# Attention scores with 64 rows of contraction for each head, and a changed row maximum, scale computation and order, in a fused attention and mixture kernel

## The chip, the cores and the metric

The kernel runs on one core of a Trainium2 chip. The metric is the time of one execution on the device, in microseconds; the time of a version is the median of several runs.

## The reference

Inputs are q, k and v of 4 batches, 12 heads, 448 tokens and 64 channels, two vectors `g_q` and `g_k` of 64, and two pairs of weight matrices (768 x 2048 and 2048 x 768). All is float32.

```python
def rmsnorm(x, g):
    return x / sqrt(mean(x * x, -1) + 1e-6) * g

scores = 0.125 * rmsnorm(q, g_q) @ rmsnorm(k, g_k).T      # for each batch and head: 448 x 448
attn = softmax(scores)                                   # over the last axis
x = (attn @ v), heads side by side                       # 1792 tokens x 768

h = x @ w_in;   g = h * clip(h + 3, 0, 6) / 6;  y = g @ w_out       # first feed-forward
h = y @ w_in2;  g = max(h, 0) ** 2;             out = g @ w_out2    # second
```

## The kernel before

**Order of work.** The program is written out by a planner. Every piece of work is a task with a key (its wished place), one or several engines that could do it, each with a cost in ns, the tasks before it and the buffers it uses; the planner simulates the engines and writes the instructions in the order that it finds. The tables at the top (`STEPS` for the place of each pair of heads, `SCALE`, `VMAX`, `LOOK`, `FROM`, `EVERY`) set the keys, and `CLASSES` the number of buffers of each size. Each engine runs its instructions in the order written, and waits by semaphores. SP issues the DMAs.

**Attention.** The work goes by 24 pairs of heads (batch `j`, pair `p`). For each pair `norms` loads q and k of both heads side by side, 128 partitions x 14 rows of 64 (`qk`), squares them (`sq`), sums the squares (`ss`), makes 1/rms on POOL (`rs`), multiplies (L509, L513) and splits the result in two float16 numbers, a high half (L526 on ScalarE, L530 on VectorE) and a low half that is the rest (L534). Both go to `src`, where each row of 128 columns is 64 high and 64 low. A DMA transpose turns `src` into `T`: on partitions 0 to 63 the high halves, on 64 to 127 the low halves, the tokens along the columns. `W` is a copy of the queries' part of `T` with the two halves of partitions exchanged, by two DMAs (L610, L611). For the first pair the transposes are three: `W` comes from a third one (L562) of a copy of `src` in reversed order.

The scores of a pair are 2 x 448 rows, in seven blocks of 128 rows. A block takes two matmuls over 128 contraction rows, `T` with `T` (high by high and low by low) and `W` with `T` (high by low and low by high), L722. The block in the middle holds rows of both heads, 64 of each, and takes two matmuls for each half. VectorE takes the negative row maximum of the block from PSUM (L729) and multiplies it by a factor `esc` (L739; after each block in batch 0, after two in the others, `GROUP`). ScalarE takes the exponential with `esc` as scale and this as bias, and sums the rows (L682). In eleven pairs of the first two batches (`ACROSS`) TensorE then transposes the exponentials in float32 (L692), they are copied back (L699) and multiplied by v in float32 (L799). In the others they are split in high and low halves (L753, L759), transposed by DMA (L767) and multiplied by v's halves in float16 (L818). The result, split again, is `x`.

**Feed-forward.** The first one runs on the 448 tokens of a batch at a time, in units of 18 matmuls of 128 x 128 by 448 columns (L1192, three float16 products for each float32 one), with the gate by L1224, L1227, L1256 and L1262. The second runs on two batches at a time, by seven products over sums of blocks (L1446, L1536). Weights are loaded, split, scaled and stored in a scratch area in DRAM, from which they are read again.

**Scales.** Before a split a value is multiplied by a power of two. `scale_of` makes it: the maximum of a column over partitions (by a TensorE transpose, L362, and a reduce, L365), its exponent kept by a mask and a floor (`pow2_floor`, L338, L339), the two factors from it (L369, L370), spread to all partitions by a small matmul (L373) and kept by a copy on either engine (L376, L379). There are 37 of these.

## Time and profile before

| what | before |
|---|---|
| median of 3 runs | 1136.13 us (1133.94 to 1138.83) |
| profiled execution | 1130.28 us, of which the span of the trace is 1128.5 |
| TensorE busy | 1050.0 us (93%), mean granted clock 0.985 |
| VectorE busy | 893.3 us (79%) |
| ScalarE busy | 770.7 us (68%) |
| GpSimd (POOL) busy | 102.2 us (9%) |

The profile is of one execution, a little under the median. Busy times are shares of the whole span and mix stretches with different limits; the rows below show them by stretch. A matmul's duration is longer than its distance to the next one, since matmuls are pipelined: distances between starts tell its cost. The same holds, less strongly, for VectorE.

### The profile page before, as it was taken

To read this page: it belongs to the slowest core of one execution; us is meant where nothing else is said; L and a number is where in the kernel's file an instruction comes from. 1 tells how busy PE (TensorE), PEld (TensorE's weight loads), DVE (VectorE), ACT (ScalarE), POOL (GpSimd) and SP (SyncE) were. 2 spreads that over 40 slices of the span, in tenths; PEclk is the share of its full clock that TensorE was granted. 3 is DMA by queue.
4 is the path that set the end of the run, shared out by engine and by line. 5 is a ranking of instruction groups with operands and counts; after the bars stand their busy time and mean duration, and the time that the engine had idled before them with its cause. 6 is when DMAs were issued, how large, how long until landed. Compare 5 with 4: busy or idle time off the path is not lost.

```text
span 1128.5 us, 17054 instructions
## 1 busy us (share of the span) xinstructions
PE 1050.0 (93%) x5765; PEld 542.5 (48%) x5765; DVE 893.3 (79%) x1952; ACT 770.7 (68%) x1480; POOL 102.2 (9%) x143
## 2 busy tenths in 40 slices
PE   1589999889999999999999999999889999999998
PEld 0255555435544554445445445454444545555554
DVE  6999989999999977799669989887889961116940
ACT  1799779899699756577458867787865656564620
POOL 3411211202202220021000000000000000000000
PEclk9699999899999999999999999999999999999999
DMA  9965557669999999999998899888765654323343
GB/s 244 248 174 175 133 168 257 188 186 272 297 284 228 242 242 208 253 222 213 200 330 312 302 317 353 307 262 273 242 201 166 225 189 126 116 91 128 113 161 105
DMA packets 235719, 246.90 MB, mean 219 GB/s; under 512 B 139392, under 2 KB 188672, under 8 KB 235632
## 3 DMA queue, kind: packets, MB, share of 16 engines
q1 hardware_dynamic: 235568, 245.68, 75.1%
q8 instruction: 45, 0.74, 0.3%
q14 instruction: 42, 0.34, 0.1%
q0 software_dynamic: 64, 0.13, 0.1%
HBM read 162.76 MB, written 45.61 MB: 185 GB/s over the span
## 4 chain that ended last, share of the span: by engine, by line
PE 54%; DVE 25%; DMA 10%; ACT 6%; issue 3%; SPq 1%; POOL 1%; ACTq 0%; DVEq 0%
PE m L1192 19%; PE ps_s L722 3%; DVE nm L729 3%; PE mo_0A L1536 2%; PE ps_a L799 2%; PE mo_1A L1536 2%; PE mo_2A L1536 2%; PE ps_s L692 2%; DMA spill_o<-wc_out 2%; DVE wc_in L1010 2%; PE mo_2C L1536 2%; DVE g L1262 2%; DMA qk<-in_qk_dram 2%; DVE wc_out L1010 1%; PE ps_r L785 1%
## 5 line engine op out<-in xcount | busy, mean ns | idle before, releaser
L1192 PEld LDWEIGHTS <-ws 128*128 128x128 f16 x2304 | 221.8, 98 | 225.5 <-issue 20.0
L1192 PE MATMUL m<-x,ws 128*128 128x448 f16 x1152 | 236.1, 355 | 7.7 <-DVE gr L1227 5.4
L1192 PE MATMUL m<-g,ws 128*128 128x448 f16 x1152 | 235.8, 354 | 6.7 <-DMA ws<-spill 4.4
L1446 PEld LDWEIGHTS <-wi 128*128 128x128 f16 x1008 | 98.8, 98 | 97.2 <-issue 5.7
L1536 PEld LDWEIGHTS <-wo 128*128 128x128 f16 x1008 | 98.3, 98 | 98.1 <-issue 5.4
L682 ACT ACTIVATE e<-ps_s,nm,esc 128x448 f32<-128x448 f32 x168 | 121.2, 724 | 26.3 <-DVE nm L739 24.7
L729 DVE TENSOR_REDUCE nm<-ps_s 128x1 f32<-128x448 f32 x168 | 102.4, 614 | 3.1 <-PE ps_s L722 2.8
L1483 ACT ACTIVATE go<-gq,g_s 128x448 f16<-128x448 f32 x104 | 62.7, 658 | 39.8 <-DVE gq L1499 27.1
L1489 DVE SCALAR_TENSOR_TENSOR go<-gq,g_s,go 128x448 f16<-128x448 f32 x112 | 71.1, 676 | 0.7 <-ACT go L1483 0.5
L692 PE MATMUL ps_s<-eye,e 128*112 128x128 f32 x308 | 49.1, 292 | 16.5 <-ACT e L682 16.1
L722 PE MATMUL ps_s<-T 128*128 128x448 f16 (+1 forms) x192 | 62.8, 377 | 0.2 <-DVE w_s L379 0.2
L722 PE MATMUL ps_s<-T,W 128*128 128x448 f16 (+1 forms) x192 | 62.3, 371 | 0.5 <-DMA W<-T 0.5
L759 DVE SCALAR_TENSOR_TENSOR p<-e,su,p 128x448 f16<-128x448 f32 x91 | 59.1, 677 | 2.1 <-ACT p L753 1.8
L1224 ACT ACTIVATE t<-m,half,six 128x448 f32<-128x448 f32 x64 | 45.6, 719 | 18.3 <-PE m L1192 18.0
L475 POOL TENSOR_TENSOR rs<-ss,mhalf 128x14 f32<-128x14 f32 x21 | 57.5, 2738 | 1.8
L753 ACT ACTIVATE p<-e,su 128x448 f16<-128x448 f32 x73 | 46.4, 663 | 12.4 <-DVE su L668 4.3
L692 PEld LDWEIGHTS ps_s<-eye,e 128*112 128x112 f32 x308 | 35.6, 140 | 36.7 <-ACT e L682 28.3
L1462 ACT ACTIVATE gq<-gq 128x448 f32<-128x448 f32 x56 | 31.9, 570 | 21.1 <-DVE gq L1391 20.6
L1536 PE MATMUL mo_0A<-go,wo 128*128 128x448 f16 x192 | 42.0, 352 | 4.3 <-DVE go L1489 4.3
L1227 DVE SCALAR_TENSOR_TENSOR gr<-t,m 128x448 f32<-128x448 f32 x64 | 39.0, 611 | 8.2 <-ACT t L1224 8.1
L1256 ACT ACTIVATE g<-gr,d 128x448 f16<-128x448 f32 x62 | 39.8, 665 | 6.6 <-DVE gr L1227 6.5
L474 POOL TENSOR_SCALAR ss<-ss 128x14 f32<-128x14 f32 x21 | 7.9, 374 | 388.8 <-DVE ss L445 334.2
(329 smaller groups left out, 1950.4 us busy)
## 6 DMA issues: line engine op xcount, KB each, us to landing
ws<-spill SPq DMA_DIRECT2D x66, 384.0 KB, 4.8
wi<-spill_i SPq DMA_DIRECT2D x48, 384.0 KB, 3.8
wo<-spill_o SPq DMA_DIRECT2D x42, 384.0 KB, 3.2
wr<-in_w1i_dram SPq DMA_DIRECT2D x16, 768.0 KB, 4.9
wr_in<-in_w2i_dram SPq DMA_DIRECT2D x16, 768.0 KB, 6.7
...
```

Source lines behind the costliest of these rows:

```text
L475: nc.gpsimd.tensor_tensor(r, ss, mhalf, op=ALU.pow)
L682: nc.scalar.activation(tl(ve)[:, r % 2], tl(vps)[:, 0:S], AF.Exp, bias=sums["nm"][:, r:r + 1], scale=esc, accum_out=sums["su"][:, r:r + 1])
L692: nc.tensor.transpose(o[:, c], tl(ve)[:, r % 2, c * VR:(c + 1) * VR], eye)
L722: nc.tensor.matmul(ps[at:at + z - a, 0:S], q_[:, a:z], ks[:, h * S:(h + 1) * S], start=(i == 0), stop=(i == 1))
L729: nc.vector.tensor_reduce(sums["nm"][:, r:r + 1], tl(vps)[:, 0:S], axis=AX.X, op=ALU.max, negate=True)
L753: nc.scalar.activation(tl(vp)[:, r % 2, 0], tl(ve)[:, r % 2], AF.Copy, scale=sums["su"][:, r:r + 1])
L759: nc.vector.scalar_tensor_tensor(tl(vp)[:, r % 2, 1], tl(ve)[:, r % 2], sums["su"][:, r:r + 1], tl(vp)[:, r % 2, 0], op0=ALU.mult, op1=ALU ...
L1192: nc.tensor.matmul(tl(vph)[:, 0:S], w[:, wa, k], tl(rhs[k])[:, xa], start=(first_ and k == 0 and c == 0), stop=(last and k == nf - 1 and c ...
L1446: nc.tensor.matmul(tl(vph)[:, 0:S], w[:, wa, k0 + k], tl(vo)[:, to, xa], start=(starts and k == 0 and x == 0), stop=(k == KH - 1 and x == ...
L1483: nc.scalar.activation(tl(vo)[:, 0], tl(v_), AF.Copy, scale=up)
L1489: nc.vector.scalar_tensor_tensor(tl(vo)[:, 1], tl(v_), up, tl(vo)[:, 0], op0=ALU.mult, op1=ALU.subtract)
L1536: nc.tensor.matmul(tl(vph)[:, 0:S], w[:, g, wa, kk], tl(ops[y])[:, xa], start=(starts and k0 + k + y == 0 and z == 0), stop=(k0 + k + y == ...
```

## The change

**Scores.** `src` and `T` now hold the high halves and the low halves in 1024 columns each, and the two heads of a pair lie on partitions 0 to 63 and 64 to 127. A score block contracts the 64 rows of its head in three matmuls: high by high, high by low, low by high (low by low is left out). Two blocks of 128 rows, one of each head, are one task of six matmuls into two PSUM tiles; the last group has 64 rows of each head in one tile. There is no `W`, and the first pair has two transposes. A transpose moves 2048 columns where it moved 1792.

```diff
+        full = n // P
+        rows = [[(h, i * P, i * P + P, 0, i * P)] for i in range(full) for h in range(2)] + [[(h, full * P, n, h * D, full * P) for h in range(2)]]
...
-            def swap():
-                nc.sync.dma_start(tl(vW)[0:D], tl(vT)[D:P, 0:NR])
-                nc.sync.dma_start(tl(vW)[D:P], tl(vT)[0:D, 0:NR])
...
-                for h, a, z, at, _ in rows[r]:
-                    for i, q_ in enumerate(qs):
-                        nc.tensor.matmul(ps[at:at + z - a, 0:S], q_[:, a:z], ks[:, h * S:(h + 1) * S], start=(i == 0), stop=(i == 1))
...
+                    for i, (qa, ka) in enumerate(((0, 0), (0, 1), (1, 0))):
+                        for x in pair:
+                            for h, a, z, at, _ in rows[x]:
+                                e = slice(h * D, h * D + D)
+                                q0 = 8 * P * qa + (MAIN + P + D if h else MAIN + 2 * P if a < MAIN else -MAIN)
+                                k0 = 8 * P * ka + (D if h else P)
+                                nc.tensor.matmul(tl(vpss[x])[at:at + z - a, 0:S], T[e, q0 + a:q0 + z], T[e, k0:k0 + S], start=(i == 0), stop=(i == 2))
```

To fill the new `src`, the split writes four pieces for a pair where it wrote one: two of 2 x 3 x 64 = 384 columns and two of 2 x 64 = 128 (the last rows are written twice).

```diff
-            s, x = flat_src()
-            nc.vector.tensor_tensor(s[:, :, D:P], x, s[:, :, 0:D], op=ALU.subtract)
...
+            for x, hi, l in pieces(t0, t1):
+                nc.vector.tensor_tensor(l, x, hi, op=ALU.subtract)
```

**Row maximum.** One instruction now reads the score tile, multiplies it by `esc` (which has become negative), writes the product back over the tile and keeps the minimum of each row. The multiplication of the maximum is gone, and the exponential takes a constant scale of -1. All 168 blocks go this way, and each instruction is followed by one that reads the accumulator.

```diff
-                nc.vector.tensor_reduce(sums["nm"][:, r:r + 1], tl(vps)[:, 0:S], axis=AX.X, op=ALU.max, negate=True)
+                x = tl(vps)[:, 0:S]
+                nc.vector.tensor_tensor_reduce(x, x, nought.to_broadcast([P, S]), esc, 3e38, ALU.add, ALU.min, sums["nm"][:, r:r + 1])
...
-                nc.vector.tensor_scalar(nm, nm, esc, None, op0=ALU.mult)
...
-                nc.scalar.activation(tl(ve)[:, r % 2], tl(vps)[:, 0:S], AF.Exp, bias=sums["nm"][:, r:r + 1], scale=esc, accum_out=sums["su"][:, r:r + 1])
+                nc.scalar.activation(tl(ve)[:, r % 2], tl(vps)[:, 0:S], AF.Exp, bias=sums["nm"][:, r:r + 1], scale=-1.0, accum_out=sums["su"][:, r:r + 1])
```

**Scales.** Both factors come from one instruction (a mask, and an exclusive or with a constant pair), and the product with another constant pair, on VectorE, takes the place of the copy. The floor is a constant column beside the values, set once on POOL. Where a scale is for a sum (`total`), two instructions stay ahead of it.

```diff
-            pow2_floor(pw, a)
-            nc.vector.tensor_scalar(pair[:, 0:1].bitcast(I32), pw.bitcast(I32), -1, (268 - shift) << 23, op0=ALU.mult, op1=ALU.add)
-            nc.vector.tensor_scalar(pair[:, 1:2], pw, 2.0 ** (shift - 14), None, op0=ALU.mult)
+                nc.vector.tensor_scalar(a, a, 2.0 ** -87, None, op0=ALU.max)
+            nc.vector.scalar_tensor_tensor(pair.bitcast(I32), a.bitcast(I32).to_broadcast([1, 2]), 0x7F800000, flip2.bitcast(I32), op0=ALU.bitwise_and, op1=ALU.bitwise_xor)
...
-        def keep_a():
-            nc.scalar.copy(box[:, 1:3], tl(vps)[:, P:P + 2])
...
-            nc.vector.tensor_copy(box[:, 1:3], tl(vps)[:, P:P + 2])
+            nc.vector.tensor_tensor(box[:, 1:3], tl(vps)[:, P:P + 2], by2[shift], op=ALU.mult)
```

**Smaller parts.** The maxima of v are taken over 128 partitions x 1344 columns where it was 112 x 1536; the low half of v of a pair is one instruction where it was two; the factor of the norms' vectors is made behind the first sum of squares.

**Order.** All numbers of the tables are new, the costs of some tasks too (the exponential 640 where 704 stood), and there is one buffer of class A less and two of class H less.

```diff
-SCALE = (0.9368554078568024, 1.125097042654467, 0.5862702874871, 0.7879065098910517)
+SCALE = (1.0381251219859378, 0.7855009702768905, 0.198882525895536, 2)
...
-CLASSES = {"A": 14, "H": 50, "B": 3, "wr": 3, "w": 8, "ps": 8}
+CLASSES = {"A": 13, "H": 48, "B": 3, "wr": 3, "w": 8, "ps": 8}
```

How the rows stand on TensorE at the first scores of the program, pair 0_0 (`ps_s_0_0_0` is its block 0, and the last number of a name is that of the value). Before:

```order
L722 LDWEIGHTS T_0_0_249
L722 MATMUL ps_s_0_0_0_304<-T_0_0_249 128x448
L722 LDWEIGHTS W_0_0_257
L722 MATMUL ps_s_0_0_0_304<-T_0_0_249,W_0_0_257 128x448
L722 LDWEIGHTS T_0_0_249
L722 MATMUL ps_s_0_0_1_307<-T_0_0_249 128x448
L722 LDWEIGHTS W_0_0_257
L722 MATMUL ps_s_0_0_1_307<-T_0_0_249,W_0_0_257 128x448
```

The same place in the changed program:

```order
L690 LDWEIGHTS T_0_0_287
L690 MATMUL ps_s_0_0_0_346<-T_0_0_287 128x448
L690 LDWEIGHTS T_0_0_287
L690 MATMUL ps_s_0_0_1_348<-T_0_0_287 128x448
L690 LDWEIGHTS T_0_0_287
L690 MATMUL ps_s_0_0_0_346<-T_0_0_287 128x448
L690 LDWEIGHTS T_0_0_287
L690 MATMUL ps_s_0_0_1_348<-T_0_0_287 128x448
L690 LDWEIGHTS T_0_0_287
L690 MATMUL ps_s_0_0_0_346<-T_0_0_287 128x448
L690 LDWEIGHTS T_0_0_287
L690 MATMUL ps_s_0_0_1_348<-T_0_0_287 128x448
```

Block 0 and block 1 (one of each head) now alternate, and each takes three matmuls where it took two of twice the contraction rows.

On VectorE, at the first row maxima of pair 0_0 (`nm` holds the maxima; `qk_0_2` and `src_0_2` belong to the norms of pair 0_2). Before:

```order
L729 TENSOR_REDUCE nm_0_0_323<-ps_s_0_0_0_304 128x1
L513 TENSOR_TENSOR qk_0_2_233<-qk_0_2_233,gg_70 128x448
L445 TENSOR_REDUCE ss_0_3_332<-sq_0_3_321 128x14
L739 TENSOR_SCALAR nm_0_0_323<-nm_0_0_323,esc_73 128x1
L729 TENSOR_REDUCE nm_0_0_323<-ps_s_0_0_1_307 128x1
L534 TENSOR_TENSOR src_0_2_334<-qk_0_2_233,src_0_2_334 128x14x64
L739 TENSOR_SCALAR nm_0_0_323<-nm_0_0_323,esc_73 128x1
```

In the changed program:

```order
L699 ISA ps_s_0_0_0_346,nm_0_0_374<-ps_s_0_0_0_346,nought_76,esc_73 128x448
L699 ISA nm_0_0_374 128x1
L512 TENSOR_TENSOR qk_0_2_275<-qk_0_2_275,rs_0_2_318 128x896
L699 ISA ps_s_0_0_1_348,nm_0_0_374<-ps_s_0_0_1_348,nought_76,esc_73 128x448
L699 ISA nm_0_0_374 128x1
L516 TENSOR_TENSOR qk_0_2_275<-qk_0_2_275,gg_70 128x448
```

The product with `esc` no longer stands some instructions behind the maximum; the reading of the accumulator stands directly behind each.

On ScalarE, ahead of the gate of unit 5 of the first feed-forward's first batch (`t_5`; `e_1_3_0` is an exponential of pair 1_3, `ws`, `wf`, `wr` are weights in work). Before:

```order
L973 ACTIVATE ws_9_1912<-wf_9_1527,w0_8_s_123 128x768
L526 CAST src_1_5_1924<-qk_1_5_1757 128x14x64
L682 ACTIVATE e_1_3_0_1929,su_1_3_1849<-ps_s_1_3_0_1834,nm_1_3_1848,esc_73 128x448
L682 ACTIVATE e_1_3_0_1929,su_1_3_1849<-ps_s_1_3_1_1837,nm_1_3_1848,esc_73 128x448
L1224 ACTIVATE t_5_1950<-m_5_1851,half_75,six0_140 128x448
```

In the changed program:

```order
L644 ACTIVATE e_1_2_0_1797,su_1_2_1751<-ps_s_1_2_0_1737,nm_1_2_1750 128x448
L933 ACTIVATE ws_8_1809<-wf_8_1466,w0_8_s_127 128x768
L933 ACTIVATE ws_9_1821<-wf_9_1516,w0_8_s_127 128x768
L644 ACTIVATE e_1_2_0_1797,su_1_2_1751<-ps_s_1_2_1_1739,nm_1_2_1750 128x448
L1184 ACTIVATE t_4_1833<-m_4_1768,half_75,six0_144 128x448
L862 ACTIVATE wr_10_1497<-wr_10_1497 128x768
L872 ACTIVATE wf_10_1831<-wr_10_1497 128x768
L862 ACTIVATE wr_11_1602<-wr_11_1602 128x768
L1184 ACTIVATE t_5_1862<-m_5_1800,half_75,six0_144 128x448
```

The gate of unit 5 now stands behind the first exponentials of pair 1_2, where it stood behind those of pair 1_3.

## Rows read from the trace of the kernel before

**Rows 1.** Busy time by stretch: length, five engines (instructions), granted clock, DMA share, GB/s.

```profile
0.00:60.00 60.00, 24.87 (x101) 12.62 (x101) 48.81 (x105) 29.92 (x58) 22.23 (x35) 0.83 0.89 232
60.00:300.00 240.00, 221.25 (x1321) 121.00 (x1320) 227.34 (x544) 206.92 (x411) 40.61 (x54) 0.98 0.70 206
300.00:690.00 390.00, 381.08 (x2132) 192.08 (x2131) 333.00 (x758) 277.93 (x517) 39.41 (x54) 1.00 0.99 263
690.00:1129.00 439.00, 422.76 (x2218) 216.83 (x2216) 284.16 (x548) 255.91 (x496) 0.00 (x0) 1.00 0.56 185
```

**Rows 2.** Waits of the run: who waits for whom, us in total, times, longest.

```profile
ACT e L682 <- DVE nm L739: 24.7, 24, 3.5
...
PE m L1192 <- DVE gr L1227: 5.4, 1, 5.4
```

**Rows 3.** Timeline of TensorE from 396 us: start, duration, instruction.

```profile
396.10 0.54 PE L1192 MATMUL m<-g,ws 128*128 128x448 f16 x2
396.48 0.35 PE L722 MATMUL ps_s<-T 128*128 128x448 f16 x1
396.67 0.35 PE L722 MATMUL ps_s<-T,W 128*128 128x448 f16 x1
396.86 0.35 PE L1192 MATMUL m<-g,ws 128*128 128x448 f16 x1
```

**Rows 4.** Timeline of TensorE around a value product of halves.

```profile
343.08 1.31 PE L1192 MATMUL m<-x,ws 128*128 128x448 f16 x6
344.31 0.38 PE L818 MATMUL ps_a<-pt_1A,v 128*64 128x448 f16 x1
344.32 0.38 PE L818 MATMUL ps_a<-pt_1B,v 128*64 128x448 f16 x1
344.53 0.35 PE L818 MATMUL ps_a<-pt_1A,v 128*64 128x448 f16 x1
...
346.23 0.35 PE L818 MATMUL ps_a<-pt_1B,v 128*64 128x448 f16 x1
346.52 0.36 PE L1192 MATMUL m<-x,ws 128*128 128x448 f16 x1
```

**Rows 5.** Groups of VectorE by form: out<-in and count, then busy us, mean ns.

```profile
L729 DVE TENSOR_REDUCE nm<-ps_s 128x1 f32<-128x448 f32 x168 | 102.4, 614 | 3.1 <-PE ps_s L722 2.8
L759 DVE SCALAR_TENSOR_TENSOR p<-e,su,p 128x448 f16<-128x448 f32 x91 | 59.1, 677 | 2.1 <-ACT p L753 1.8
L534 DVE TENSOR_TENSOR src<-qk,src 128x896 f16<-128x896 f32 x23 | 24.9, 1081 | 2.3 <-ACT src L526 2.3
L1065 DVE TENSOR_TENSOR wq_in<-wq_in 128x384 f32<-128x384 f32 x32 | 17.7, 554 | 0.4
...
L1459 DVE SCALAR_TENSOR_TENSOR gq<-gq 128x448 f32<-128x448 f32 x8 | 5.0, 621 | 0.0
L1459 DVE DVE_READ_ACCUMULATOR gq<-gq 128x1 f32 x8 | 0.7, 85 | 0.0
```

**Rows 6.** Timeline of VectorE from 114 us: a row bias, a row maximum, the next.

```profile
114.35 0.21 DVE L739 TENSOR_SCALAR nm<-nm,esc 128x1 f32<-128x1 f32 x1
114.47 0.61 DVE L729 TENSOR_REDUCE nm<-ps_s 128x1 f32<-128x448 f32 x1
115.01 1.08 DVE L445 TENSOR_REDUCE ss<-sq 128x14 f32<-128x896 f32 x1
```

**Rows 7.** Timeline of VectorE from 24 us: the steps of a scale, the next.

```profile
24.38 0.14 DVE L338 TENSOR_SCALAR v_s<-v_s 1x1 int32<-1x1 int32 x1
...
24.86 1.06 DVE L445 TENSOR_REDUCE ss<-sq 128x14 f32<-128x896 f32 x1
```

**Rows 8.** Groups of ScalarE by form, as in Rows 5.

```profile
L682 ACT ACTIVATE e<-ps_s,nm,esc 128x448 f32<-128x448 f32 x168 | 121.2, 724 | 26.3 <-DVE nm L739 24.7 <-PE ps_r L785 0.9
...
L526 ACT CAST src<-qk 128x896 f16<-128x896 f32 x19 | 17.8, 935 | 15.1 <-DVE qk L513 15.1
L1300 ACT ACTIVATE yr<-m,ov 128x448 f32<-128x448 f32 x19 | 11.9, 625 | 8.1 <-PE m L1192 8.1
```

**Rows 9.** Timeline from 21 us: the third transpose, the first score.

```profile
21.30 1.24 SPq L562 DMA_TRANSPOSE W<-W_0r  x1
...
25.50 0.55 PE L722 MATMUL ps_s<-T 128*128 128x448 f16 x1
```

**Rows 10.** DMA issues: count, KB each, median us from issue to landing.

```profile
W<-T SPq DMA_DIRECT2D x46, 112.0 KB, 3.5
```

More of the change, by code (lines that the diff above doesn't have):

```diff
@@ L84, with twice @@
 CUT = 2
+TTR = 30
 LAG = 16
-CLASSES = {"A": 14, "H": 50, "B": 3, "wr": 3, "w": 8, "ps": 8}
+CLASSES = {"A": 13, "H": 48, "B": 3, "wr": 3, "w": 8, "ps": 8}
 SHIFT = 2
 GUESTS = (
-    (("qk", "sq", "src", "T", "v", "v16", "e", "p16"), 14),
-    (("qk", "sq", "src", "T", "v", "v16"), 14),
-)
+    (("qk", "sq", "src", "T", "v", "v16", "e", "p16"), 13),
+    (("qk", "sq", "src", "T", "v", "v16"), 13),
+)
+def twice(x, step):
+    n, d = x.shape[-1], x.shape[-1] - step
+    return bass.AP(x.tensor, x.offset, [*x.ap[:-1], [step, 2], [1, d]])
 class Value:
@@ L329, in tile_kernel @@
     half = cst.tile([P, 1], F32, tag="half", name="half")
+    nought = cst.tile([P, 1], F32, tag="nought", name="nought")
     ones = cst.tile([1, P], F32, tag="ones", name="ones")
     column1 = cst.tile([P, 1], F32, tag="column1", name="column1")
+    flip2 = cst.tile([1, 2], F32, tag="flip2", name="flip2")
+    by2 = {x: cst.tile([P, 2], F32, tag=f"by{x}", name=f"by{x}") for x in (0, SHIFT)}
     kept = dram.tile([len(PAIRS), KC, P, 2, S], F32, name="kept")
@@ L359, in row @@
             if total:
-                nc.tensor.matmul(tl(vps)[0:1, 0:FC], column1, vals(), start=True, stop=True)
+                nc.tensor.matmul(tl(vps)[0:1, 0:len_], column1, vals(), start=True, stop=True)
             else:
@@ new lines, in norms, with of, sq_a @@
+        cuts = ((0, NR), (NR, 2 * NR)) if fast else ((0, 2 * NR),)
+        tqs = [task(k0 - (22 - .1 * a) * sc, [("SP", 420, lambda c=c: load_q(*c))], [] if fast else early, [vq], xfer=(c[1] - c[0]) * 92) for a, c in enumerate(cuts)]
+        vsq = val("sq", j, p, -18 * sc)
+        def of(v_, t0, t1):
+            x = tl(v_)
+            return x.rearrange("p a t -> p (a t)")[:, t0 * D:t1 * D]
+        def sq_a(t0, t1):
+            nc.scalar.activation(of(vsq, t0, t1), of(vq, t0, t1), AF.Square)
@@ L585, in norms, with pieces @@
-        prep[b, p] = vT, t_trs, vW, t_w
+        def pieces(t0, t1):
+            x, y = tl(vq), tl(vsrc)
+            out = []
+            for w in range(t0 // NR, t1 // NR):
+                at, e0, step = ((MAIN + 2 * P, 0, MAIN + P + D), (P, D, MAIN + D))[w]
+                src = x[:, w * NR:w * NR + 2 * NB + 2].rearrange("p (h b) d -> p h b d", h=2)[:, :, 0:NB]
+                out.append((src, *(y[:, z, at:at + MAIN].rearrange("p (b h d) -> p h b d", b=NB, h=2) for z in range(2))))
+                src = x[:, w * NR + NB:w * NR + NB + 1].to_broadcast([P, 2, D])
+                out.append((src, *(y[:, z, e0:e0 + step + D].rearrange("p x -> p x") for z in range(2)), step))
+            return [(o[0], *(ap if len(o) == 3 else twice(ap, o[3]) for ap in o[1:3])) for o in out]
@@ new lines, in hi_a, with hi_v, lo, tr @@
+        def hi_a(t0, t1):
+            for x, hi, _ in pieces(t0, t1):
+                nc.scalar.copy(hi, x)
+        def hi_v(t0, t1):
+            for x, hi, _ in pieces(t0, t1):
+                nc.vector.tensor_copy(hi, x)
+        def lo(t0, t1):
+            for x, hi, l in pieces(t0, t1):
+                nc.vector.tensor_tensor(l, x, hi, op=ALU.subtract)
+        vT = val("T", j, p, -14.6 * sc)
+        def tr(z0, z1):
+            at, y = tl(vT)[:, z0 * 8 * P:z1 * 8 * P], tl(vsrc)[:, z0:z1].rearrange("p z x -> p (z x)")
+            nc.sync.dma_start_transpose(out=at.rearrange("p (b e) -> p b e", e=P), in_=y)
@@ L588, in attention @@
+        t_trs = []
+        for z in ((0, 1), (1, 2)) if fast else ((0, 2),):
+            dep = t_his if z[1] == 1 else t_los
+            t_trs.append(task(k0 - (14.6 - .02 * z[0]) * sc, [("SP", 1800, lambda z=z: tr(*z))], dep, [vsrc, vT], xfer=1700 if fast else 2000))
+        first.append(t_trs[-1])
+        prep[b, p] = vT, t_trs
     def attention(j, p, k0, sc):
@@ L852, in tile_kernel @@
     vscale = {}
-    vmx = [lasting(2, f"vm{b}") for b in range(B)]
+    vmx = [guarded(2, f"vm{b}") for b in range(B)]
     def largest(b, k):
@@ L875, in tile_kernel @@
     stored, wscale = {}, {}
-    wsum, t_sums = lasting(FC, "wsum"), []
+    wsum, t_sums = lasting(3 * FC // TWIN, "wsum"), []
+    floors.extend(wsum[:, x:x + 1] for x in range(2, 3 * FC // TWIN, 3))
     iwi = [lasting(FC, f"iwi{m}") for m in range(2)]
@@ L1020, in sums @@
         name = f"{kind}{r}"
-        mx = lasting(2 * len(parts), f"w2m_{name}")
+        mx = guarded(2 * len(parts), f"w2m_{name}")
         made, t_ms = [], []
```

288 lines of the change are left out of this document (112 added, 176 removed).

## The prediction

> **What bounds the kernel now.** I read the busy time by stretches first. From 60 to 300 us VectorE works 227.3 of 240 us (95%) and TensorE 221.3 (92%), so VectorE sets the pace there and TensorE stands idle for 18.7 us. From 300 to 690 us TensorE works 381.1 of 390 us and VectorE 333.0, and from 690 us TensorE 422.8 of 439 us and VectorE only 284.2: there TensorE sets the pace. The first 60 us are start-up, with TensorE busy for 24.9 us [rows 1]. The waits say the same: the longest single stall of TensorE between 60 and 300 us is one of 5.4 us for VectorE's `gr`, and ScalarE waits 24 times, 24.7 us in all, for the row bias that VectorE makes after each row maximum [rows 2]. So three rules price the edits. VectorE work taken away before 300 us gives time back, up to TensorE's 18.7 us of slack. TensorE work added before 300 us costs nothing while that slack lasts, and added after 300 us it costs its full length. VectorE or ScalarE work taken away after 300 us gives nothing but a shorter wait.
>
> **The change part by part.**
>
> *Scores on TensorE.* Before, a row block takes two matmuls that start 0.19 us apart, and the first MoE matmul follows 0.19 us behind: 396.48 to 396.86 us is 0.38 us for one block, with no gap at either end [rows 3]. A pair of heads has six such blocks and one block in two halves of 64 columns, which lie side by side in two steps. That makes 24 x (12 + 2) x 0.19 = 63.8 us. Now two blocks (one of each head) share three steps: 24 x (3 x 3 + 3) x 0.19 = 54.7 us, if the two heads run side by side. That saves 9.1 us. No row shows two tiles of 64 rows by 128 columns side by side. The nearest are the two halves of the value product, 64 columns each: they start 0.01 us apart, and ten steps take from 344.31 to 346.23 us, 0.19 each [rows 4]. I take that. The other end is one head behind the other, 0.38 a step: 54.7 us more.
>
> The same rows price the change of tile shape. The last of the six MoE matmuls starts near 344.03 us (five steps of 0.19 after 343.08), so the first narrow one comes after 0.28 us where 0.19 is usual, and the step after it takes 0.22. On the way out, 346.23 to 346.52 us is 0.29 where 0.19 is usual [rows 4]. So a change of shape costs about 0.095 us and a stretch 0.03 us more. Before, only the 24 half blocks (and the value products) change shape. Now all scores do: in the program's order the changes on TensorE go from 257 to 373, and the score stretches in a narrow shape from 24 to 94. 116 x 0.095 + 70 x 0.03 = 13.1 us. The net is +4.0 us of TensorE work; nothing, if row tiles change shape for free, would make it -9.1.
>
> For two row tiles I have a rule that speaks against full overlap: the Trainium skill, TensorE: Matmul & The Clock Gate, in Part 3 (Measured speedup vs the span model), gives 3.07 times for four row tiles, not four times. With that share a step would take an estimated 0.25 us instead of 0.19, and the 288 steps 17 us more. The trace's 64-column tiles show no such loss, and no run here shows 64-row tiles; the sum goes by the rows.
>
> *Row maximum and row bias.* Before: 168 reduces of 614 ns [rows 5] and 114 small multiplies (in batch 0 after each reduce, later after two). An instruction's duration overlaps the next: a bias's successor starts 0.12 us after it, a reduce's 0.54 us after it [rows 6]. So 168 x 0.54 + 114 x 0.12 = 104.4 us. Now 168 instructions read the score tile and a constant, write the tile back scaled, and keep the minimum; each is followed by one that reads the accumulator. The two nearest rows: an instruction over 448 columns with an accumulator lasts 621 ns (like the reduce) and its accumulator read 85 ns; one whose factor comes from a tile lasts 677 ns, 63 more than the reduce [rows 5]. Between 0.54 and 0.60 + 0.085 us, so 91 to 115 us; I take 0.57 (the read starts as the next does), 95.8 us: -8.6 us, between -13 and +11. The exponential no longer waits for a bias, and in batches 1 to 3 no longer for the second row of two.
>
> *Other VectorE work.* The four small steps of a scale take from 24.38 to 24.86 us [rows 7]; one step of perhaps 0.15 is left of them: 37 x 0.33 = -12.2, of which ten copies that ScalarE made and the four maxima kept give 1.8 back: -10.4. The low halves were one instruction of 1081 ns; now they are two of 384 columns and two of 128. 384 columns last 554 ns [rows 5], 0.47 net, and 128 by the same slope 0.20: 1.34 against 1.00, 24 times: +8.2. The values' low halves in one piece, shorter maxima of V and one copy of `W` less: -3.6. In all -14.4 us of 893. Of these parts, about half the row maxima and the scales, somewhat more of the low halves and all maxima of V lie before 300 us: about -6.5 us.
>
> *ScalarE.* The exponential's scale is a constant now. With two factors from tiles it lasts 724 ns, an activation with one 625 [rows 8]: up to -13 us. The high halves are four pieces instead of one of 935 ns [rows 8]: two of about 0.42 and two of about 0.22 net against 0.84, 22 times: +10. It cancels, and ScalarE has slack.
>
> *The copies of T.* 46 transfers of 112 KB that land 3.5 us after issue [rows 10] and their 46 issues on SP go; the transposes become 2048 columns for 1792. What was queued behind them on SP (weight loads) moves up. TensorE waits little for `W` itself; I take -1.0 us.
>
> *Start.* The third transpose, which waits for the reversed copy, is issued at 21.30 us, and the first score starts at 25.50 [rows 9]. Now two transposes go; the low halves of the first pair still wait behind one maximum of V on VectorE (its row stands between theirs), so the second is issued about 0.9 us earlier: -0.9.
>
> *Order.* On ScalarE, at unit 5 the program before stands at pair 1_3, now at pair 1_2: VectorE has one pair less to do (about 8 us) ahead of that unit. Batch 1 must still be done before its own units, so most of this comes back by 300 us. Between 0 and -8, I take -2.
>
> **The sum** in the profiled execution: -0.9 (start) - 6.5 (VectorE before 300 us) - 2 (order) + 2.0 (the half of TensorE's 4.0 that lies after 300 us) - 1.0 (`W`) = -8.4 us. 1128.5 becomes 1120.1 us of span. That execution took 1130.28 us, 5.85 below the median of the runs, so the median becomes 1136.13 - 8.4 = 1127.7 us.
>
> **The rivals.**
>
> *The heads run one behind the other, or overlap in part* (slower). In favour: no row shows such tiles. Against: column tiles overlap in full. Half an overlap adds 27 us of TensorE work and none 55; before 300 us the slack of 18.7 us hides some, so 1150 to 1180 us. It decides from a step of 0.24 us on: 288 x 0.05 = 14 us, more than the 8.4 won. The share of 3.07 in 4 of the page named above would be just there.
>
> *The relief is idle time* (no change). If what VectorE saves before 300 us is only work that the new order puts back ahead of the same units, and TensorE's four microseconds count in full, the sum is -0.9 + 4.0 - 1.0: 1138 us. In favour: TensorE is at 92% there already. Against: its longest stall is on VectorE.
>
> *The new order fills the stalls* (clearly faster). If TensorE's 18.7 us of idle time between 60 and 300 us shrink by two thirds and a few microseconds of the start go too: -20 us, 1114 to 1118 us.
>
> **How the numbers follow.** The forecast (1118 to 1135 us) has 0.50; 0.44 of it lies under 1130.4. The heads not side by side 0.16, all slower. Idle relief 0.20, of which 0.15 within 0.5% and 0.05 slower. Filled stalls 0.14. Half a percent, 5.7 us, is about what a measurement of this kernel can tell from no change. So faster 0.58, same 0.06 + 0.15 = 0.21, slower 0.16 + 0.05 = 0.21. The range takes the low end of the unknown prices (row maximum -13, shapes free, order -8: about -25) and, above, the dearest row maximum and a part of an overlap: 1109 to 1150 us. The forecast's own range is 1118 to 1135.
>
> **What would show it.** Score matmuls of two heads that start some 0.01 us apart, with steps of 0.19 us and 0.28 us at a change of shape. A row maximum of 0.54 to 0.60 us to its successor. VectorE's busy time near 880 us, TensorE's idle time from 60 to 300 us nearer 10 than 19 us, and from 300 us on as dense as now. The first score near 24.6 us. Steps of 0.25 us or more, or VectorE no less busy, would make the prediction wrong.

## The result, and the profile after

| | before | after |
|---|---|---|
| median | 1135.27 us (1133.94 to 1138.83, 4 runs) | 1124.04 us (1121.79 to 1124.78, 4 runs) |
| ratio | | 0.9893, 95% interval 0.9865 to 0.9920 |
| median, measured again | 1132.58 us (1127.95 to 1137.88, 23 runs) | 1125.83 us (1121.97 to 1130.02, 12 runs) |
| ratio | | 0.9939, 95% interval 0.9922 to 0.9957 |
| span of the trace | 1128.5 us, again 1130.3 | 1122.8 us, again 1123.3 |

The change makes the kernel 7 to 11 us faster; 8.4 was forecast. The two intervals don't overlap, and no run tells why. The traces of the two versions differ by 6 to 7 us, and it is this difference that they can explain. The windows of the changed kernel, with the columns of [rows 1]:

```profile
0.00:60.00 60.00, 28.76 (x177) 14.86 (x179) 52.64 (x126) 34.65 (x84) 23.71 (x71) 0.94 0.71 226
60.00:300.00 240.00, 223.94 (x1423) 114.32 (x1421) 221.15 (x543) 213.87 (x447) 37.78 (x54) 0.97 0.71 214
300.00:690.00 390.00, 373.19 (x2147) 180.14 (x2144) 328.63 (x776) 267.59 (x518) 39.16 (x54) 0.99 0.97 255
690.00:1123.00 433.00, 421.33 (x2218) 216.25 (x2216) 280.30 (x528) 247.54 (x477) 0.00 (x0) 1.00 0.56 181
```

Read against [rows 1], TensorE's idle time (length less busy time) goes from 35.1 to 31.2 us at the start, from 18.7 to 16.1 us up to 300 us, **up** from 8.9 to 16.8 us between 300 and 690 us, and from 15.7 to 11.5 us behind that (up to the spans' ends). With 2.8 us less of busy time (1050.0 to 1047.2) this is -3.9 - 2.7 + 7.9 - 4.2 - 2.8 = -5.7 us, the whole difference between the spans. VectorE's busy time falls from 893.3 to 882.7 us.

Windows of fixed times hold different work in the two programs. The matmuls of the two feed-forwards are the same in number, so the same one can be looked up in both traces: the first of the first feed-forward, the first output product of the second one (`mo_0A`), and the first of its second two batches (`mi_0A`). Before:

```profile
92.91 0.74 PE L1192 MATMUL m<-x,ws 128*128 128x448 f16 x3
...
830.14 0.92 PE L1536 MATMUL mo_0A<-go,wo 128*128 128x448 f16 x4
...
915.35 0.93 PE L1446 MATMUL mi_0A<-yo,wi 128*128 128x448 f16 x4 [0.72 <-DMA wi<-spill_i]
```

In the changed kernel:

```profile
83.97 0.73 PE L1152 MATMUL m<-x,ws 128*128 128x448 f16 x3
...
828.56 0.35 PE L1496 MATMUL mo_0A<-go,wo 128*128 128x448 f16 x1 [0.19 <-ACT go L1443]
...
909.75 0.92 PE L1406 MATMUL mi_0A<-yo,wi 128*128 128x448 f16 x4
```

The first feed-forward begins 8.9 us earlier. From there to the second one's first output product it takes 744.6 us for 737.2, 7.4 more. The next part takes 81.2 us for 85.2, 4.0 less, and the rest is equal. In the second pair of traces the three are -9.1, +5.8 and -3.6 us. TensorE's longest wait in the third part is one for VectorE's `go`. From 690 us on, before and in the changed kernel:

```profile
PE mo_0A L1536 <- DVE go L1489: 4.3, 3, 2.8
...
PE mo_0A L1496 <- DVE go L1449: 2.4, 4, 0.8
```

What TensorE newly waits for between 300 and 690 us stands in the waits of the changed kernel between 380 and 560 us and in the DMA view of 420 to 500 us (the queue's packets, MB and packet time as a share of 16 engines; T's transposes, median us from issue to landing):

```profile
PE ps_s L690 <- DMA T<-src: 7.3, 2, 4.4
```

```profile
q1 hardware_dynamic: 36260, 18.92, 106.8%
...
T<-src SPq DMA_TRANSPOSE x4, 5.8
```

The same rows of the kernel before:

```profile
q1 hardware_dynamic: 35013, 18.01, 100.6%
...
T<-src SPq DMA_TRANSPOSE x3, 4.5
```

Both kernels fill the DMA engines there, and the changed one waits for its transposes: the two of T that TensorE waits for are issued at 444.75 and 473.93 us, and land 5.3 and 9.1 us later. That the full engines make them late is likely, but no run takes transfers out of this stretch. Before 300 us, VectorE's `gr` no longer stalls TensorE for 5.4 us [rows 2]; in its place stands a stall of 6.1 us for ScalarE's exponentials.

The scores, in the timeline of TensorE (a run of equal matmuls is one row):

```profile
501.33 3.00 PE L1152 MATMUL m<-x,ws 128*128 128x448 f16 x15
504.26 1.43 PE L690 MATMUL ps_s<-T 64*64 64x448 f16 x12
505.62 1.12 PE L1152 MATMUL m<-x,ws 128*128 128x448 f16 x5
```

Twelve matmuls of two groups, one of 64 x 64 and one of 64 x 128 tiles, take from 504.26 to 505.62 us, 1.36 us: six steps of 0.19 are 1.14, and two changes of shape (between the groups, and behind them) add 0.1 each. The fifteenth MoE matmul started at 501.33 + 14 x 0.19 = 503.99, and the first score came 0.27 us behind it. So the heads run side by side in full, as forecast from [rows 3, 4].

VectorE's and ScalarE's groups by form, as in [rows 5, 8]:

```profile
L699 DVE CUSTOM_DVE_ANT_0 ps_s<-ps_s,nought,esc 128x448 f32<-128x448 f32 x168 | 113.5, 683 | 10.0 <-PE ps_s L690 9.8
L541 DVE TENSOR_TENSOR src<-qk,src 128x384 f16<-128x384 f32 x48 | 26.4, 549 | 0.1
...
L699 DVE DVE_READ_ACCUMULATOR2_ANT nm<- 128x1 f32 x168 | 23.4, 139 | 0.0
...
L541 DVE TENSOR_TENSOR src<-qk,src 128x128 f16<-128x128 f32 x48 | 13.6, 282 | 0.0
```

```profile
L644 ACT ACTIVATE e<-ps_s,nm 128x448 f32<-128x448 f32 x168 | 106.5, 636 | 18.8 <-DVE nm L699 10.2 <-DVE p L718 3.4 <-DVE y_s L371 1.4
...
L533 ACT CAST src<-qk 128x384 f16<-128x384 f32 x44 | 22.9, 520 | 15.9 <-DVE qk L512 10.1 <-DVE qk L516 2.0 <-DVE su L630 1.9
L533 ACT CAST src<-qk 128x128 f16<-128x128 f32 x44 | 13.6, 308 | 0.0
```

The row maximum lasts 683 ns, as long as the dearer of its two neighbours in [rows 5] (677). What it costs up to its successor, and a scale, in the timeline of VectorE:

```profile
19.60 0.27 DVE L380 TENSOR_REDUCE v_s<-v_p 1x1 f32<-1x128 f32 x1
19.91 0.15 DVE L384 SCALAR_TENSOR_TENSOR v_s<-v_s,flip 1x2 int32<-1x2 int32 x1
19.98 0.15 DVE L485 TENSOR_SCALAR ss<-ss 128x14 f32<-128x14 f32 x1
...
110.89 0.67 DVE L699 CUSTOM_DVE_ANT_0 ps_s<-ps_s,nought,esc 128x448 f32<-128x448 f32 x1
111.50 0.13 DVE L699 DVE_READ_ACCUMULATOR2_ANT nm<- 128x1 f32 x1
111.50 0.61 DVE L805 TENSOR_TENSOR x<-xr,x 128x448 f16<-128x448 f32 x1
```

The read of the accumulator starts with the next instruction. The maximum takes 0.61 us here to its successor; the median of the 161 that nothing else holds up is 0.60, the shortest 0.56. The one step of a scale takes 0.07 us where the four took 0.48 [rows 7].

### The profile page after: what moved, and what is told of

It is laid out like the page before. It is cut to its first block, busy times and chain, and to the rows that moved or that the text cites. A ratio compares the mean times of both kernels' runs of the same rounds, so it can differ in the third digit from the quotient of the medians.

```text
span 1122.8 us, 17421 instructions
## 1 busy us (share of the span) xinstructions
PE 1047.2 (93%) x5957; PEld 525.6 (47%) x5957; DVE 882.7 (79%) x1970; ACT 763.6 (68%) x1522; POOL 100.6 (9%) x179
## 4 chain that ended last, share of the span: by engine, by line
PE 46%; DVE 29%; DMA 13%; ACT 5%; issue 3%; SPq 2%; POOL 1%; ACTq 0%; DVEq 0%
PE m L1152 11%; DVE ps_s L699 4%; PE mo_2A L1496 3%; PE mo_1A L1496 3%; PE mo_0A L1496 3%; DMA spill_o<-wc_out 3%; PE ps_s L690 2%; DMA spill_i<-wc_in 2%; PE ps_a L758 2%; PE ps_s L654 2%; DVE src L541 2%; PE mo_2C L1496 2%; PE mo_1C L1496 2%; DVE wc_in L970 2%; PE mo_0C L1496 2%
## 5 line engine op out<-in xcount | busy, mean ns | idle before, releaser
L1152 PEld LDWEIGHTS <-ws 128*128 128x128 f16 x2304 | 217.6, 98 | 219.7 <-issue 29.9
L1152 PE MATMUL m<-g,ws 128*128 128x448 f16 x1152 | 231.5, 353 | 2.6 <-DMA ws<-spill 1.3
L699 DVE CUSTOM_DVE_ANT_0 ps_s<-ps_s,nought,esc 128x448 f32<-128x448 f32 x168 | 113.5, 683 | 10.0 <-PE ps_s L690 9.8
L644 ACT ACTIVATE e<-ps_s,nm 128x448 f32<-128x448 f32 x168 | 106.5, 636 | 18.8 <-DVE nm L699 10.2
L690 PE MATMUL ps_s<-T 64*128 64x448 f16 (+1 forms) x576 | 75.4, 372 | 10.4 <-DMA T<-src 9.5
L654 PE MATMUL ps_s<-eye,e 128*112 128x128 f32 x308 | 51.6, 301 | 18.8 <-ACT e L644 18.6
L690 PEld LDWEIGHTS <-T 64*128 64x128 f16 (+1 forms) x576 | 22.2, 100 | 50.6 <-issue 32.8
L1222 DVE SCALAR_TENSOR_TENSOR g<-gr,d,g 128x448 f16<-128x448 f32 x64 | 42.4, 675 | 0.4 <-ACT g L1216 0.2
```

Source lines behind the costliest of these rows:

```text
L644: nc.scalar.activation(tl(ve)[:, r % 2], tl(vps)[:, 0:S], AF.Exp, bias=sums["nm"][:, r:r + 1], scale=-1.0, accum_out=sums["su"][:, r:r + 1])
L654: nc.tensor.transpose(o[:, c], tl(ve)[:, r % 2, c * VR:(c + 1) * VR], eye)
L690: nc.tensor.matmul(tl(vpss[x])[at:at + z - a, 0:S], T[e, q0 + a:q0 + z], T[e, k0:k0 + S], start=(i == 0), stop=(i == 2))
L699: nc.vector.tensor_tensor_reduce(x, x, nought.to_broadcast([P, S]), esc, 3e38, ALU.add, ALU.min, sums["nm"][:, r:r + 1])
L1152: nc.tensor.matmul(tl(vph)[:, 0:S], w[:, wa, k], tl(rhs[k])[:, xa], start=(first_ and k == 0 and c == 0), stop=(last and k == nf - 1 and c ...
```

## The experiments

All are timed against the kernel before, whose median was 1132.6 to 1132.7 us in the three sets; the changed kernel's was 1125.8 in the first of them. "Slower" or "faster than the changed kernel" goes by this second measurement of it. By the intervals of the two ratios such a difference is uncertain by 3 to 4 us, and against the first measurement's ratio each kernel would stand 5 us slower.

**1. Both kernels again.**

> The kernel before, unchanged, for a second trace. The profiled execution of before took 1130.28 us, under all its other runs (1133.94 to 1138.83). If that execution was an exception, this one takes 1133 to 1139 us and its trace shows where the 4 to 8 us more lie; if the traces of before are always that fast, it takes 1129 to 1131 us and the change is worth only 5 to 6 us between traces.

Measured: one execution of 1132.1 us, span 1130.3, between the two ranges and of the same shape: TensorE idle for 18.4 us between 60 and 300 us and 10.2 us from 300 to 690. In 23 further executions the kernel takes 1127.95 to 1137.88 us, so the first trace (1130.28) was not an exception.

> The changed kernel, unchanged, for a second trace and a tighter interval. By the theory that the lead of the first 430 us is always lost between 430 and 545 us, where the DMA engines are at their limit, the unit at 545 us starts again within 2 us of where it starts in the trace of before, and the time is 1122 to 1125 us. By the rival, that the loss there was an accident of one execution, part of the lead (5 to 15 us) is still there at 545 us and the time is below 1120 us.

Measured: 1125.83 us, ratio 0.9939 (0.9922 to 0.9957). The second trace shows the same: TensorE busy for 372.4 of 390 us between 300 and 690 us, so 17.6 us idle. The matmul that starts at 545.0 and 546.0 us in the traces of before (the 1441st of the first feed-forward) starts at 545.5 and 543.7 in those of the changed kernel. The loss there is no accident of one execution.

**2. Edits and tables exchanged.**

```diff
-SCALE = (1.0381251219859378, 0.7855009702768905, 0.198882525895536, 2)
+SCALE = (0.9368554078568024, 1.125097042654467, 0.5862702874871, 0.7879065098910517)
...
```

> All edits of the change, with the tables of places and times of the kernel before (buffers and task costs as in the change). If the gain comes from the edits, 1122 to 1129 us, and the first unit of the first feed-forward starts some 5 us earlier than in the kernel before (92.9 us). If it comes from the new tables, 1133 us or more.

Measured: 1137.92 us (10 runs), ratio 1.0058 (1.0034 to 1.0082): the edits under the old tables make the kernel slower, though the first feed-forward starts at 84.3 us in it, as early as in the changed kernel.

> The kernel before with the changed kernel's tables of places and times (buffers, task costs and the grouping of the row bias as before). If the gain comes from the edits, 1133 us or more. If it comes from the tables, 1122 to 1128 us. Both this and the opposite exchange above 1135 us would mean that tables and edits only work together.

Measured: 1158.55 us, ratio 1.0233 (1.0199 to 1.0268). The first feed-forward starts at 90.3 us. Both halves alone lose, 5 and 26 us, and together they win 7. Each of the two mixtures has its stalls in other places. TensorE's waits in the edits under the old tables, from 686 to 840 us:

```profile
PE mo_0A L1496 <- DVE go L1449: 5.7, 2, 5.3
PE mi_0A L1406 <- DVE gq L1348: 3.2, 1, 3.2
PE mi_7A L1406 <- DVE gq L1348: 2.7, 2, 2.5
```

and in the old edits under the new tables, over the whole run:

```profile
PE ps_a L818 <- DMA pt_5B<-p: 13.4, 2, 8.9
```

So each mixture has single stalls of 5 to 9 us that the changed kernel has not. These runs read as if tables and durations fit only each other. What "the order" is worth by itself has no answer here.

**3. One head behind the other.**

```diff
-                    for i, (qa, ka) in enumerate(((0, 0), (0, 1), (1, 0))):
-                        for x in pair:
-                            for h, a, z, at, _ in rows[x]:
+                    for x in pair:
+                        for h, a, z, at, _ in rows[x]:
+                            for i, (qa, ka) in enumerate(((0, 0), (0, 1), (1, 0))):
```

> The changed kernel with the three matmuls of one head ahead of the three of the other, all else in the same order. In the trace of the changed kernel two heads start 0.004 us apart and a step lasts 0.19 us. If that overlap needs neighbours from different rows, a group of six now takes about 1.1 us instead of 0.57, TensorE has 48 to 55 us more work, and since its idle time is 75 us in all and mostly tied to waits, the time is 1150 to 1175 us. If the tiles overlap in any order, nothing changes (1122 to 1127 us).

Measured: 1125.22 us, ratio 0.9930 (0.9903 to 0.9956): nothing lost. The timeline of TensorE in this kernel:

```profile
504.79 0.92 PE L1152 MATMUL m<-x,ws 128*128 128x448 f16 x4
505.65 0.75 PE L690 MATMUL ps_s<-T 64*128 64x448 f16 x6
506.33 0.74 PE L1152 MATMUL m<-x,ws 128*128 128x448 f16 x3
```

Six matmuls take 0.68 us, three steps of 0.19 and a change of shape, though the three of one head stand ahead of the three of the other in the program. The overlap doesn't hang on which of these two orders the program has. The experiment therefore did not price TensorE's time; number 7 does.

**4. Row maximum as before.**

```diff
+        nc.vector.tensor_scalar(esp, gsc[:, 0:1], 0.125 * 2.0 * 2.0 ** -24, None, op0=ALU.mult)
...
-                nc.vector.tensor_tensor_reduce(x, x, nought.to_broadcast([P, S]), esc, 3e38, ALU.add, ALU.min, sums["nm"][:, r:r + 1])
+                nm = sums["nm"][:, r:r + 1]
+                nc.vector.tensor_reduce(nm, x, axis=AX.X, op=ALU.max, negate=True)
+                nc.vector.tensor_scalar(nm, nm, esp, None, op0=ALU.mult)
...
-                nc.scalar.activation(tl(ve)[:, r % 2], tl(vps)[:, 0:S], AF.Exp, bias=sums["nm"][:, r:r + 1], scale=-1.0, accum_out=sums["su"][:, r:r + 1])
+                nc.scalar.activation(tl(ve)[:, r % 2], tl(vps)[:, 0:S], AF.Exp, bias=sums["nm"][:, r:r + 1], scale=esp, accum_out=sums["su"][:, r:r + 1])
```

> The changed kernel with the row maximum as it was: a reduce (0.53 us to its successor) and a multiplication by a factor (0.12, or up to 0.21 where it waits for the reduce), and the exponential with a factor from a tile again (0.61 us to its successor where the constant scale has 0.52). The order written out is the same. VectorE has 168 x 0.055 to 0.14 = 9 to 24 us more, ScalarE 15 us more. If VectorE and ScalarE set the pace before 300 us and that time stays to the end, about a half of the larger one is lost: 1130 to 1138 us. If the lead of that stretch is lost between 380 and 545 us anyway, less than 4 us is: 1122 to 1128 us.

Measured: 1137.38 us, ratio 1.0031 (1.0013 to 1.0050), 11.6 us slower than the changed kernel. Its windows:

```profile
0.00:60.00 60.00, 26.76 (x158) 13.65 (x159) 52.08 (x120) 33.34 (x75) 23.74 (x71) 0.94 0.71 219
60.00:300.00 240.00, 216.41 (x1380) 108.90 (x1379) 222.85 (x523) 214.10 (x434) 38.62 (x54) 0.97 0.69 204
300.00:690.00 390.00, 373.15 (x2146) 178.54 (x2144) 338.31 (x786) 276.86 (x526) 38.88 (x54) 0.99 0.95 250
690.00:1135.00 445.00, 433.01 (x2279) 222.44 (x2277) 291.24 (x547) 255.71 (x490) 0.00 (x0) 1.00 0.58 188
```

Up to 300 us TensorE gets 9.5 us less done (243.2 of busy time for 252.7), while VectorE is about as busy (274.9 us for 273.8). That loss stays to the end: the span is 12.0 us longer. The whole run has 904.5 us of VectorE time, 21.8 more, and 780.0 us of ScalarE time, 16.4 more, and does not tell the two apart. The multiplication that directly follows its reduce makes this dearer than the row bias of the kernel before was, so it gives no more than an upper end of the price. A second version comes nearer to the row bias of before:

```diff
...
+            def rowbias(r0=rows_[0][0], r1=r + 1):
+                nm = sums["nm"][:, r0:r1]
+                nc.vector.tensor_scalar(nm, nm, esc, None, op0=ALU.mult)
+
+            t_mx = task(kk + .5 * sc, [("DVE", 126, rowbias)], [t_mx])
...
```

> The changed kernel with the row maximum of before as it was there: a reduce, the multiplication as a piece of work of its own (after each block in batch 0, after two in the others), the exponential with a factor from a tile, and the old costs for the three; tables and all else of the change stay. In the run with a multiplication directly behind each reduce that step waited for the reduce (0.65 us from the reduce to it where 0.53 is usual), so that run overstated the price. If VectorE's work is what counts, 168 x 0.534 + 114 x 0.125 = 104 us stand against 101 now, and the kernel is 1 to 2 us slower: 1126 to 1128 us. If ScalarE's shorter exponential (15.5 us in all, more than half of it before 300 us) and the missing step between maximum and exponential count, 4 to 8 us slower: 1130 to 1134 us.

Measured: 1153.47 us, ratio 1.0189 (1.0154 to 1.0223), beyond both theories. With the old costs the planner wrote another order, and TensorE's longest wait in it is one for a transpose of the last step of a pair's attention:

```profile
PE ps_a L787 <- DMA pt_5A<-p: 18.4, 1, 18.4
```

This run says nothing of the row maximum; it repeats number 2.

**5. Long steps of the scales.**

```diff
-                nc.vector.tensor_scalar(a, a, 2.0 ** -87, None, op0=ALU.max)
-            nc.vector.scalar_tensor_tensor(pair.bitcast(I32), a.bitcast(I32).to_broadcast([1, 2]), 0x7F800000, flip2.bitcast(I32), op0=ALU.bitwise_and, op1=ALU.bitwise_xor)
+            nc.vector.tensor_scalar(pw.bitcast(I32), a.bitcast(I32), 0x7F800000, None, op0=ALU.bitwise_and)
+            nc.vector.tensor_scalar(pw, pw, 2.0 ** -87, None, op0=ALU.max)
+            nc.vector.tensor_scalar(pair[:, 0:1].bitcast(I32), pw.bitcast(I32), -1, (268 - shift) << 23, op0=ALU.mult, op1=ALU.add)
+            nc.vector.tensor_scalar(pair[:, 1:2], pw, 2.0 ** (shift - 14), None, op0=ALU.mult)
...
-            nc.vector.tensor_tensor(box[:, 1:3], tl(vps)[:, P:P + 2], by2[shift], op=ALU.mult)
+            nc.vector.tensor_copy(box[:, 1:3], tl(vps)[:, P:P + 2])
```

> The changed kernel with the four small steps of a scale instead of one, all else in the same order: VectorE has 37 x 0.33 = 12 us more, about half of it before 300 us. If VectorE sets the pace there and what is lost there stays, 3 to 6 us slower than the changed kernel (1129 to 1132 us). If the steps fall into its waits, within 1.5 us.

Measured: 1132.01 us, ratio 1.0004 (0.9984 to 1.0024), 6.2 us slower than the changed kernel. VectorE is busy for 893.4 us, 10.7 more: 0.58 us of time for each. ScalarE is not touched (764.6 us for 763.7). But TensorE's waits for the factors, ahead of the small matmuls that spread them, rise from 5.3 to 10.1 us, so a part of the price is the length of a chain that TensorE waits for, and not VectorE's load.

**6. The small low pieces on GpSimd.** The same question with the other sign, and a version that might beat both.

```diff
-            for x, hi, l in pieces(t0, t1):
-                nc.vector.tensor_tensor(l, x, hi, op=ALU.subtract)
+            for i, (x, hi, l) in enumerate(pieces(t0, t1)):
+                (nc.gpsimd if i % 2 and not fast else nc.vector).tensor_tensor(l, x, hi, op=ALU.subtract)
```

> The changed kernel with the two small low pieces of a pair (128 columns each, 0.20 us to the successor on VectorE) on GpSimd for 23 pairs: VectorE has 46 x 0.20 = 9 us less, half of it before 300 us. If VectorE sets the pace there, 2 to 5 us faster than the changed kernel (1121 to 1123 us). If GpSimd takes long over a piece, or stands behind its own waits, T comes later and the kernel is as fast or up to 5 us slower.

Measured: 1121.46 us (1119.96 to 1124.20, 6 runs), ratio 0.9900 (0.9872 to 0.9929), 4.4 us faster than the changed kernel by its second measurement, though the two intervals overlap a little; against the first (0.9893) it is no gain. Its span, 1118.2 us, is 4.6 us shorter than the changed kernel's. GpSimd's group by form:

```profile
L541 POOL TENSOR_TENSOR src<-qk,src 128x128 f16<-128x128 f32 x46 | 29.9, 658 | 141.8 <-ACT src L533 103.4 <-issue 19.3 <-DVE src L537 7.6
```

A piece takes 658 ns there and 282 ns on VectorE (the Trainium skill, GPSIMD Engine Reference, in 4.1 Engine selection, warns of a factor of about 2 for two operands and names VectorE for such work; the factor, 2.3 here, agrees with this row, and this kernel did not lose by going against the advice). VectorE is busy for 876.6 us, 6.2 less: 0.71 us of time for each.

Where experiments 4 to 6 part from the changed kernel shows at the 17th of the first feed-forward's 64 gates, in the changed kernel, then in the first version of 4, in 5 and in 6:

```profile
291.03 0.72 ACT L1184 ACTIVATE t<-m,half,six 128x448 f32<-128x448 f32 x1
...
301.24 0.72 ACT L1188 ACTIVATE t<-m,half,six 128x448 f32<-128x448 f32 x1 [0.32 <-PE m L1156]
...
296.81 0.72 ACT L1186 ACTIVATE t<-m,half,six 128x448 f32<-128x448 f32 x1
...
288.13 0.72 ACT L1184 ACTIVATE t<-m,half,six 128x448 f32<-128x448 f32 x1
```

There they are 10.2 and 5.8 us late and 2.9 us early; the spans end 12.0 and 10.3 us late and 4.6 us early. So more than half of each difference arises before 300 us, and the stretch with the full DMA engines behind it makes nothing good.

**7. Late scores twice.**

```diff
-                    for i, (qa, ka) in enumerate(((0, 0), (0, 1), (1, 0))):
+                    terms = ((0, 0), (0, 1), (1, 0))
+                    for i, (qa, ka) in [*enumerate(terms)] * (2 if b > 1 else 1):
```

> The changed kernel, with each score group of batches 2 and 3 computed twice into the same tile (the second time from the start): 12 pairs x 12 steps x 0.19 us = 27 us more for TensorE after 300 us, nothing more for any other engine or queue. By the rule of the prediction, that TensorE work after 300 us costs its full length, 25 to 28 us slower than the changed kernel: 1150 to 1154 us. If the transposes by DMA set the pace from 380 to 500 us, a part vanishes in TensorE's idle time of 13 us there: 1138 to 1146 us.

Measured: 1142.91 us, ratio 1.0081 (1.0052 to 1.0110), 17.1 us slower than the changed kernel (20.0 between the spans), of 27.4 us of TensorE work (48 groups that take 1.24 us where they took 0.67). That is inside the second range. Its window:

```profile
300.00:690.00 390.00, 379.12 (x2312) 183.14 (x2310) 313.27 (x741) 254.55 (x495) 37.77 (x54) 0.99 0.91 233
```

TensorE's idle time in it is 10.9 us where it was 16.8, and the share of the DMA engines fell from 0.97 to 0.91.

**8. The copies of T issued again.**

```diff
...
+                    if r == 0 and (j, p) != (0, 0):
+                        nc.sync.dma_start(spare[0:D], T[D:P, 0:SPARE])
+                        nc.sync.dma_start(spare[D:P], T[0:D, 0:SPARE])
```

> The changed kernel, and for 23 pairs two copies of a part of T (108 KB each, read by nobody) are issued with the pair's first scores. If the DMA queue sets the pace from 380 to 500 us, where its engines are busy all the time and two transposes of T land 5 to 9 us late, 5 MB more in it cost 3 us or more. If dropping the copies was worth only what TensorE waited for W (0.5 us in the trace of before), the time is within 2 us of the changed kernel's.

Measured: 1128.87 us, ratio 0.9972 (0.9951 to 0.9993), 3.0 us slower than the changed kernel, about as much as the uncertainty. TensorE is busy for 369.2 us between 300 and 690 us, so 20.8 idle, 4.0 more, though no engine reads the copies. The 46 issues take SP's time too, some 0.58 us each, and the run does not tell this from the load on the DMA engines. (They stand a little later in SP's queue than `W`'s did.) In the kernel before, SP also stood still ahead of `W`'s copies until T had landed, which it does not do here:

```profile
SPq L610 <- DMA T<-src: 18.4, 9, 4.6
```

**9. The norms' factor first.**

```diff
+        norm_scale()
...
-                first_scale.append(task(k0 - 17.65 * sc, [("DVE", 1000, norm_scale)], [t_rs]))
+                first_scale.append(task(k0 - 17.65 * sc, [("DVE", 1000, lambda: None)], [t_rs]))
```

> The changed kernel with the factor of the norms' vectors made at the head of VectorE's queue again, where it waits for a small load on GpSimd's queue (7.1 us in the trace of before). The first score, at 20.6 us in the changed kernel and 25.5 before, comes 1.5 to 3 us later. If time won at the start stays to the end, the kernel is 1.5 to 3 us slower; if it is lost in the waits between 380 and 545 us, it is within 1 us of the changed kernel's, and the unit of the first feed-forward at 545 us starts within 1 us of where it starts now.

Measured: 1125.37 us, ratio 0.9932 (0.9910 to 0.9955). The first score came at 21.30 us, only 0.7 later, so the run doesn't decide what time at the start is worth; nor was a larger delay tried. The matmul that starts at 545.5 and 543.7 us in the changed kernel's two traces starts at 541.5 here, so a place there differs by some us between traces.

## Why the prediction was right

**The time** lies 3.7 us from the first median and 1.9 from the second. The forecast was -8.4 us from a base of 1136.13; 23 later executions put the kernel before at 1132.58, and the change is worth 11.2 or 6.8 us. That two heads run side by side in full is shown. That VectorE's work ahead of 300 us sets the pace, so that a part of what is taken from it comes back, is borne out by three experiments that each leave something open. The prediction took 6.5 of 14.4 us, 0.45. Experiment 6 gives 0.71 us of time for each microsecond of VectorE's busy time, experiment 5, in the other direction, 0.58 with a longer chain in it, and experiment 4 (first run) 0.53 with ScalarE's 16.4 us in it. Between the spans the three are 0.75, 0.97 and 0.55, so the rate is known only roughly. The change took 10.6 us of VectorE's time away; at 0.53 to 0.71 that is an estimated 5.6 to 7.5 us within the order that the change has. It is no account of the whole gain, since by experiment 2 the same edits lose 5 us in another order.

**VectorE's sum** came out at -10.6 us of busy time for -14.4. The low halves cost what was worked out (0.47 and 0.20 us to the successor). The row maximum was mis-sized: at 0.6 us to its successor it saves 168 x 0.6 = 101 against 104.4 us, some 3.6 us and not 8.6. The scales were about right: the four steps put back raise VectorE's busy time by 10.7 us (experiment 5), where 12.2 and, less what the change gives back, 10.4 were worked out. ScalarE's two parts were to cancel; its busy time falls from 770.7 to 763.7 us.

**TensorE's steps and shapes** were right: steps of 0.19 us for two heads, 0.27 to 0.29 us at a change of shape. Between matmuls of the first feed-forward a group of six takes 0.77 us with both changes (median of 48), where a block took 0.38 and the block in halves 0.60; 24 pairs make that 24 x (4 x 0.77 - 6 x 0.38 - 0.60) = +4.8 us for the forecast 4.0. The rival of heads one behind the other is out, even where the program puts them so, and with it the share of 3.07 in 4 of the Trainium skill (TensorE: Matmul & The Clock Gate, Part 3, Measured speedup vs the span model), which is measured there for four tiles and not for two: here three steps of two tiles and a change of shape fill the 0.68 us.

**The step that failed** is the one from 300 us on. The prediction kept the lead won before 300 us and expected the rest "as dense as now". TensorE's idle time there grew by 7.9 us, more than 0 to 300 us had gained (6.6). By the same matmuls, the first feed-forward begins 8.9 us earlier and has 1.6 us of that left when the second one's output products begin (9.1 and 3.3 in the second traces). To this extent the rival of relief that is only idle time was right. The waits name T's transposes, in a stretch in which the DMA engines are full in both kernels. Experiments 7 and 8 fit that: 27.4 us of TensorE work after 300 us cost 17 to 20 us, not their full length, and copies of T that nobody reads cost about 3. But they don't show it, and experiments 4 to 6 carry what they lose or win before 300 us through that stretch. Whether the full queue or the new order lost the lead stays open. That TensorE's idle time between 60 and 300 us would come nearer to 10 than to 19 us was wrong too: 16.1.

The sum came out because another 4.0 us (3.6) returned in the second feed-forward, where the prediction had nothing. These two errors cancel, and that is luck. The part that gave them, from `mo_0A` to the second `mi_0A`, takes 81.2 us in the nine traces that keep the change's order, whatever else is changed, 85.2 and 84.8 in the kernel before, and 87.1 to 87.9 in the kernels of experiment 2 and in the second version of experiment 4, which have other orders. So the gain belongs to the order that the planner found for the new edits, tables and costs together, and neither to the edits nor to the tables alone.

**The start** was mis-sized: the first score comes at 20.62 us, 4.9 earlier [rows 9], not 0.9. It comes with the edits and not with the order: 20.38 us in the edits under the old tables, 25.28 in the old edits under the new ones. The prediction took the third transpose for what the first score waits for. On TensorE the score stands behind two small matmuls of a scale of v, and these wait for VectorE. Before, and in the changed kernel:

```profile
23.66 0.37 PE L362 MATMUL v_p<-eye,v_s 128*1 128x128 f32 x1 [4.99 <-DVE v_s L356]
...
25.50 0.55 PE L722 MATMUL ps_s<-T 128*128 128x448 f16 x1
```

```profile
18.75 0.37 PE L377 MATMUL v_p<-eye,v_s 128*1 128x128 f32 x1 [4.41 <-DVE v_s L371]
...
20.62 0.56 PE L690 MATMUL ps_s<-T 64*128 64x448 f16 x2
```

3.4 of the 4.9 us are there already when VectorE goes on with 1/rms (11.28 us for 14.67), behind the second maximum of v, which starts at 9.81 instead of 13.00 us. 0.7 of them are the norms' factor (experiment 9); the loads of v in their new shape are the likeliest rest, which no run separates.

**The copies of T** were taken at -1.0 us; issued again they cost about 3, with an uncertainty as large. TensorE's wait for `W` (0.5 us) is not their price; the load on the DMA engines and SP's time are not told apart. **The order** was given -2 us as if it were a part like others. Experiment 2 shows that it isn't: the edits gain only with an order that fits them.
